# Local attention values with the probabilities as weights, and a feed-forward weight decode per f on VectorE

## The chip, the core and the metric

The kernel runs on one core of a Trainium2 chip. The core has five engines with queues of their own: PE (TensorE, the 128x128 matrix array; its weight loads are listed apart as PEld), VectorE (DVE), ScalarE (ACT), GpSimd (POOL), and SyncE (SP), whose queue issues every DMA of this kernel. Matrix products go to PSUM, eight banks of 128 partitions by 512 float32 columns; all else lives in SBUF. The metric is the device time of one execution in microseconds. A profile shows one execution; its span runs from the first to the last instruction.

## The reference

A batch of 8 with 8 heads of size 64 has 512 local and 32 global tokens. Global queries attend to all 544 keys; local queries attend to the 32 global keys and to local keys at most 32 positions away. The result, of all heads side by side (512 features for each of 4352 tokens), goes through a two-layer feed-forward network with 2048 hidden features.

```python
s_g = scale * np.matmul(q_g, k_all.transpose(0, 1, 3, 2))
out_g = np.matmul(sm(s_g), v_all)
s_ll = scale * np.matmul(q_l, k_l.transpose(0, 1, 3, 2))
mask = np.abs(pos[:, None] - pos[None, :]) <= 32
s_ll = np.where(mask, s_ll, -1e9)
s_lg = scale * np.matmul(q_l, k_g.transpose(0, 1, 3, 2))
a_l = sm(np.concatenate([s_lg, s_ll], axis=-1))
out_l = np.matmul(a_l, np.concatenate([v_g, v_l], axis=2))
...
h = x @ w_in
g = np.maximum(h, 0.0) + alpha * np.minimum(h, 0.0)
return (g @ w_out).astype(np.float32)
```

`sm` is a softmax whose denominator has 1e-9 added.

## The kernel before

Everything is kept transposed: features on partitions, tokens on columns. Two heads make a pair; there are 32 pairs P, four for each batch entry. The feed-forward network runs over 9 groups of tokens: the local tokens of each batch entry (512 columns), and last all global tokens (256 columns). Each group takes 16 steps f, one for each 128 hidden features, so that there are 144 steps t in all, and 10 steps of a prelude ahead of them (t from -10).

In step t, `f1(t)` forms 128 hidden features in one PSUM bank by 12 products of 128x128 weights with 512 columns. Float32 accuracy comes from splitting both factors in a high and a low part (`split`, and `wt`, which holds both parts of the weights) and adding three products. VectorE applies the slope (L291, L292), ScalarE rounds the high part `gh` (L294), GpSimd forms the low part `gl` (L295). `f2` of two steps earlier adds that step's features into four output banks: part 0 (8 products with `gh`) and part 1 (4 with `gl`). Between these stand three places for attention: "pre" ahead of f1, "mid" between f1 and f2's part 0, and "post" between f2's two parts. `plan` (L325 on) puts the attention there: for the local pair P its scores and softmax, two steps later the transposes of the probabilities, three steps later the value products; for the global queries of a pair, every 3.4 steps from t = 16, scores at "mid" of a step and transposes and values at "mid" two steps later.

For a local pair, 16 windows of 32 queries against 128 keys and two heads give 32 products with 32-wide weights (`local_scores`). `local_softmax` masks and negates (L190), takes the minimum (L191), exponentiates on ScalarE in eight pieces with the sums (L193), and multiplies by the reciprocal (L194 to L197). `local_transposes` turns the probabilities on PE and copies them to SBUF. `local_values` (L217) uses the values, 128 keys by 64 features, as weights and streams 32 turned probabilities, 32 products that alternate between the two halves of the array's columns; its result is already transposed and is copied to `x_raw` (L228). `global_values` (L258) turns the global probabilities `sg_sb` into `sgt_sb` and then adds up 5 blocks of keys for each head in one bank. A float32 product appears as two records in the trace.

The weights come as float64 and are turned into float32 bits in the kernel: `load_weights`, `decode_words` (two ScalarE steps, three VectorE steps, one addition on GpSimd, L133 to L140) and `split_weights` (a cast on ScalarE or VectorE, and a subtraction on GpSimd, L150). Of the 32 pieces of 512 columns, 5 are decoded in the prelude and two in each step from t = 0.

The program is ordered by a scheduler that models the engines' times, with priorities by program order; from t = 16 (`PIN`) PE's instructions keep the written order. Every engine and the SP queue take their instructions in order, so a waiting one holds up those behind it. Buffers: tag "s" has two PSUM banks for scores, transposes, values and all global attention from pair 4 on; "h" has two for f1; "o0" to "o3" hold the outputs. `wpool` has 33 buffers of 4 KB a partition.

Of the kernel before, what the change touches and what calls it, by code (L numbers as in the profile page):

```python
# [55 lines left out]
def longformer_ffn(ctx: ExitStack, tc: tile.TileContext, qk, vs, gn, vg, w, alpha, out):  # L56
# [66 lines left out]
    wraw, wmid, wts = {}, {}, {}  # L123

    def load_weights(f, j):
        wraw[f, j] = wpool.tile([128, 1024], U32, tag="w", name="wraw")
        nc.sync.dma_start(wraw[f, j], w[f, j].bitcast(U32))

    def decode_words(f, j):
        words = wraw.pop((f, j)).rearrange("p (n two) -> p n two", two=2)  # L130
# [9 lines left out]
        nc.gpsimd.tensor_tensor(ti, ti, r, op=ALU.add)  # L140
        wmid[f, j] = t

    def split_weights(f, j):
        t = wmid.pop((f, j))
        wt = wpool.tile([128, 2, 512], F32R, tag="w", name="wt")
        if j:
            nc.vector.tensor_copy(wt[:, 0, :], t)  # L147
# [36 lines left out]
    def local_softmax(P):  # L184
        for h in range(2):
# [4 lines left out]
            nc.vector.scalar_tensor_tensor(p, s, -0.125, mask.rearrange("q i n -> q (i n)"), op0=ALU.mult, op1=ALU.add)  # L190
            nc.vector.tensor_reduce(mn, p3, axis=AX.X, op=ALU.min)  # L191
            for i in range(4):
                nc.scalar.activation(p3[:, i], p3[:, i], AF.Exp, bias=mn[:, i : i + 1], scale=-1.0, accum_out=z[:, i : i + 1])  # L193
# [266 lines left out]
```

## Time and profile before

| | us |
|---|---|
| median of 3 runs | 1083.85 (1083.85 to 1089.67) |
| the profiled execution's own time | 1083.33 |
| its span | 1081.5 |
| PE busy, 8752 matmul instructions | 1016.3 (94%) |
| VectorE busy, 1206 instructions | 573.9 (53%) |
| ScalarE busy, 995 instructions | 338.0 (31%) |
| GpSimd busy, 227 instructions | 281.0 (26%) |

How to read the rows that follow: a row of a timeline gives the start, the length, the engine, the line, the operation, the output and inputs by the program's names, the shape and the count; in square brackets stands the idle time ahead of it and what ended it. Matmuls are pipelined and their ends are modelled, so the start of the next batch tells more than the length of one. A row of the groups gives the count, then the busy time, the mean length in ns, and the idle time. A row of the windows gives the stretch and its length, the busy time of PE, PEld, DVE, ACT and POOL with their instructions, the granted PE clock (1.00 is full), the DMA share and GB/s. L78 and L84 are helpers that issue all products and transposes, so the tile names tell them apart.

### The profile page before, as it was taken

Reading aid. Unit: us, or ns where it says so; the run is one execution under the profiler, and the core shown is the slowest. Engines: PE = TensorE matmul, PEld = TensorE weight load, DVE = VectorE, ACT = ScalarE, POOL = GpSimd, SP = SyncE. Lnnn points to the kernel's source line nnn. Section 1 sums busy time; section 2 is a strip of 40 time slices with the busy share of each in tenths; the row PEclk is TensorE's granted clock in tenths of the full one; section 3 lists DMA queues with packets and bytes.
Section 4 is the critical chain, followed back from the end, with each engine's and each line's share of the span. In section 5 each row is a group of like instructions: output and inputs, shape, how many; then the busy total and the mean of one; then the engine's idle time right before and its main releaser. Section 6 shows DMA issues by size and latency. Waiting matters only on the chain.

```text
span 1081.5 us, 21173 instructions
## 1 busy us (share of the span) xinstructions
PE 1016.3 (94%) x8752; PEld 804.9 (74%) x8752; DVE 573.9 (53%) x1206; ACT 338.0 (31%) x995; POOL 281.0 (26%) x227
## 2 busy tenths in 40 slices
PE   6899989899999999999999999999999999999998
PEld 4676566677777777777777777777777777777798
DVE  4579999844445445554454544644453444433322
ACT  3445445332223222422223222422232222311121
POOL 2248777421111121211112112112111212111222
PEclk8698898899999999999999999999999999999999
DMA  9936320243223223333223322333323211200010
GB/s 314 312 143 220 113 89 26 77 128 91 87 76 117 64 86 92 100 119 97 89 88 104 89 63 77 128 89 102 89 89 105 87 44 45 75 24 13 1 40 20
DMA packets 90416, 103.09 MB, mean 95 GB/s; under 512 B 3792, under 2 KB 69840, under 8 KB 90320
## 3 DMA queue, kind: packets, MB, share of 16 engines
q1 hardware_dynamic: 90320, 101.73, 29.9%
q8 instruction: 69, 1.13, 0.4%
q14 instruction: 27, 0.22, 0.1%
HBM read 92.81 MB, written 8.91 MB: 94 GB/s over the span
## 4 chain that ended last, share of the span: by engine, by line
PE 76%; DVE 16%; issue 3%; ACT 2%; DMA 1%; POOL 1%; SPq 0%; DVEq 0%; POOLq 0%; ACTq 0%
PE h_ps L78 31%; PE o L78 31%; PE o_ps L78 5%; DVE g L291 3%; PE pt L84 3%; DVE wt L138 2%; PE s_ps L78 2%; PE gt L78 2%; DVE wt L135 2%; PE g_ps L78 2%; DVE xl L214 1%; DVE p L190 1%; DVE wt L147 1%; DVE sgt_sb L263 1%; ACT p L193 1%
## 5 line engine op out<-in xcount | busy, mean ns | idle before, releaser
L295 POOL TENSOR_TENSOR gl<-g,gh 128x512 fp32r<-128x512 f32 (+1 forms) x144 | 186.0, 1292 | 713.5 <-ACT gh L294 489.8
L78 PE MATMUL h_ps<-xh,wt 128*128 128x512 f32 (+1 forms) x1152 | 358.0, 392 | 5.1 <-POOL wt L150 4.4
L78 PE MATMUL o<-gh,wt 128*128 128x512 f32 (+1 forms) x1152 | 281.8, 386 | 1.6 <-ACT gh L294 1.5
L291 DVE TENSOR_SCALAR g<-h_ps,alpha_sb 128x512 f32<-128x512 f32 (+1 forms) x144 | 103.6, 719 | 319.4 <-PE h_ps L78 296.0
L78 PEld LDWEIGHTS h_ps<-xh,wt 128*128 128x128 f32 x1152 | 209.0, 191 | 52.5 <-issue 8.0
L78 PEld LDWEIGHTS o<-gh,wt 128*128 128x128 f32 x1152 | 203.8, 189 | 41.9 <-ACT gh L294 2.9
L294 ACT CAST gh<-g 128x512 fp32r<-128x512 f32 (+1 forms) x144 | 85.6, 594 | 449.3 <-DVE g L292 369.8
L78 PE MATMUL h_ps<-xl,wt 128*128 128x512 f32 (+1 forms) x576 | 222.6, 387 | 2.0 <-DVE xl L214 2.0
L78 PE MATMUL o<-gl,wt 128*128 128x512 f32 (+1 forms) x576 | 148.9, 380 | 2.1 <-POOL gl L295 2.1
L193 ACT ACTIVATE p<-p,mn 128x128 f32<-128x128 f32 x256 | 99.2, 389 | 103.8 <-DVE mn L191 87.2
L78 PEld LDWEIGHTS h_ps<-xl,wt 128*128 128x128 f32 x576 | 109.9, 191 | 26.4 <-DVE xl L214 4.0
L78 PEld LDWEIGHTS o<-gl,wt 128*128 128x128 f32 x576 | 105.1, 189 | 23.6 <-POOL gl L295 3.5
L292 DVE SCALAR_TENSOR_TENSOR g<-h_ps,g 128x512 f32<-128x512 f32 (+1 forms) x144 | 94.5, 656 | 2.5
L78 PEld LDWEIGHTS o_ps<-pt,vw 128*64 128x64 f32 x2048 | 67.4, 146 | 13.9 <-issue 9.8
L78 PE MATMUL o_ps<-pt,vw 128*64 128x32 f32 x2048 | 71.2, 230 | 1.8 <-DVE pt L99 1.8
L190 DVE SCALAR_TENSOR_TENSOR p<-s_ps,mask 128x512 f32<-128x512 f32 x64 | 41.1, 683 | 49.4 <-PE s_ps L78 49.3
L140 POOL TENSOR_TENSOR wt<-wt,wr 128x512 int32<-128x512 int32 x32 | 44.3, 1385 | 63.6 <-DVE rz L194 24.4
L78 PE MATMUL s_ps<-qk 64*32 64x128 f32 x2048 | 53.3, 295 | 5.5 <-DMA qk<-in_qk_dram 3.5
L78 PE MATMUL gt<-sgt_sb,vg 128*64 128x32 f32 x640 | 24.8, 225 | 34.1 <-DVE sgt_sb L263 34.1
L78 PEld LDWEIGHTS s_ps<-qk 64*32 64x32 f32 x2048 | 35.6, 113 | 28.4 <-issue 18.0
L197 DVE TENSOR_TENSOR p<-p,rz 128x512 f32<-128x512 f32 x60 | 53.4, 891 | 1.9
L78 PEld LDWEIGHTS gt<-sgt_sb,vg 128*64 128x64 f32 x640 | 21.2, 137 | 41.7 <-DVE sgt_sb L263 41.7
(62 smaller groups left out, 752.0 us busy)
## 6 DMA issues: line engine op xcount, KB each, us to landing
vw<-in_vs_dram SPq DMA_DIRECT2D x64, 512.0 KB, 5.1
qk<-in_qk_dram SPq DMA_DIRECT2D x32, 672.0 KB, 4.1
wraw<-in_w_dram SPq DMA_DIRECT2D x32, 512.0 KB, 6.8
vg<-in_vg_dram SPq DMA_DIRECT2D x32, 320.0 KB, 2.9
gn<-in_gn_dram SPq DMA_DIRECT2D x32, 304.0 KB, 2.9
out_dram<-ost SPq DMA_DIRECT2D x32, 256.0 KB, 2.4
out_dram<-ost SPq DMA_DIRECT2D x4, 128.0 KB, 1.8
alpha_sb<-in_alpha_dram SPq DMA_DIRECT2D x1, 8.0 KB, 1.8
```

The costliest lines, as they stand in the source:

```text
L78: ins = nc.tensor.matmul(*a, **k)
L84: ins = nc.tensor.transpose(*a)
L135: nc.vector.tensor_scalar(t, t, CLAMP_LO, CLAMP_HI, op0=ALU.max, op1=ALU.min)
L138: nc.vector.scalar_tensor_tensor(tu, high, 0xC0000000, tu, op0=ALU.bitwise_and, op1=ALU.bitwise_or)
L140: nc.gpsimd.tensor_tensor(ti, ti, r, op=ALU.add)
L190: nc.vector.scalar_tensor_tensor(p, s, -0.125, mask.rearrange("q i n -> q (i n)"), op0=ALU.mult, op1=ALU.add)
L193: nc.scalar.activation(p3[:, i], p3[:, i], AF.Exp, bias=mn[:, i : i + 1], scale=-1.0, accum_out=z[:, i : i + 1])
L197: eng.tensor_tensor(p3, p3, sub_ap(rz, 0, 128, 0, ((1, 4), (0, 128))), op=ALU.mult)
L291: nc.vector.tensor_scalar(g[:, 0:n], h[:, 0:n], 0.0, alpha_sb[:, f : f + 1], op0=ALU.min, op1=ALU.mult)
L292: nc.vector.scalar_tensor_tensor(g[:, 0:n], h[:, 0:n], 0.0, g[:, 0:n], op0=ALU.max, op1=ALU.add)
L294: nc.scalar.copy(gh[:, 0:n], g[:, 0:n])
L295: nc.gpsimd.tensor_tensor(gl[:, 0:n], g[:, 0:n], gh[:, 0:n].bitcast(F32), op=ALU.subtract)
```

## The change

- Local values: the turned probabilities (32 columns) become the weights and the values (64 columns) are streamed, four windows into the four quarters of the array's columns. The result has queries on partitions; it is multiplied by the reciprocal sums there (`xq`), and four transposes in a function of its own, `local_outputs`, bring it to the old layout. The probabilities are no longer scaled. `plan` puts the values at "post" of the step of the transposes, and `local_outputs` at "mid" of the next.
- Global values: the transposes go to "pre" of the step behind the scores, the products to "post" of that step, with both heads in one product of 128-wide weights and 64 columns, of which the copies take each head's own block.
- Weights: both halves of an f are loaded, decoded and split together, 1024 columns a step, with the addition and subtraction on VectorE and the cast on ScalarE. Three f are decoded in the prelude, the others spread over t = 1 to 13.
- Prelude: 7 steps instead of 10, a pair in each; the loads of the four pairs and of three weight tiles are issued ahead, into buffers of the weight pool (17 of 8 KB now). Later pairs have one buffer instead of two for `qk` and for `v`; `gn` and `vg` share three buffers with the decode.

```diff
-NWARM = 12
+NWARM = 9
 WARM = (2, 2)
-NWB = 33
-NST = 22
+NWB = 17
+NST = 21
 ...
-NPRE = 10
+NPRE = 7
 PIN = 16
+PAD = (176, 32)
 LAG = 2
-AHEAD = 6
-EARLY = 6
+NDEC = 3
 ...
-    wraw, wmid, wts = {}, {}, {}
-
-    def load_weights(f, j):
-        wraw[f, j] = wpool.tile([128, 1024], U32, tag="w", name="wraw")
-        nc.sync.dma_start(wraw[f, j], w[f, j].bitcast(U32))
-
-    def decode_words(f, j):
-        words = wraw.pop((f, j)).rearrange("p (n two) -> p n two", two=2)
+    wslot, wmid, wts = {}, {}, {}
+
+    def wide(name, dtype=F32):
+        return work.tile([128, 1024], dtype, tag="dec", name=name, bufs=3)
+
+    def load_weights(f):
+        wslot[f] = wpool.tile([128, 2048], U32, tag="w", name="ws")
+        nc.sync.dma_start(wslot[f], w[f].bitcast(U32))
+
+    def decode_words(f):
+        words = wslot.pop(f).rearrange("p (n two) -> p n two", two=2)
         low, high = words[:, :, 0], words[:, :, 1]
-        t, r = stage("wt"), stage("wr", I32)
+        t, r = wide("wt"), wide("wr", I32)
 ...
         ti = t.bitcast(I32)
-        nc.gpsimd.tensor_tensor(ti, ti, r, op=ALU.add)
-        wmid[f, j] = t
-
-    def split_weights(f, j):
-        t = wmid.pop((f, j))
-        wt = wpool.tile([128, 2, 512], F32R, tag="w", name="wt")
-        if j:
-            nc.vector.tensor_copy(wt[:, 0, :], t)
+        nc.vector.tensor_tensor(ti, ti, r, op=ALU.add)
+        wmid[f] = t
+
+    def split_weights(f):
+        t = wmid.pop(f).rearrange("p (j n) -> p j n", j=2)
+        wt = wpool.tile([128, 2048], F32R, tag="w", name="wt").rearrange("p (j s n) -> p j s n", j=2, s=2)
+        nc.scalar.copy(wt[:, :, 0, :], t)
+        nc.vector.tensor_tensor(wt[:, :, 1, :], t, wt[:, :, 0, :].bitcast(F32), op=ALU.subtract)
+        for j in range(2):
+            wts[f, j] = wt[:, j]
+
+    qks, vws = {}, {}
+
+    def load_qk(P):
+        if P < NPAIR:
+            qks[P] = wpool.tile([128, 2048], F32, tag="w", name="qk")[:, 0 : SL + KS]
         else:
-            nc.scalar.copy(wt[:, 0, :], t)
-        nc.gpsimd.tensor_tensor(wt[:, 1, :], t, wt[:, 0, :].bitcast(F32), op=ALU.subtract)
-        wts[f, j] = wt
-
-    qks, vws = {}, {}
-
-    def load_qk(P):
-        qks[P] = work.tile([128, SL + KS], F32, tag="qk", name="qk", bufs=2)
+            qks[P] = work.tile([128, SL + KS + PAD[1]], F32, tag="qk", name="qk", bufs=1)[:, 0 : SL + KS]
         nc.sync.dma_start(qks[P], qk[P])
 
     def load_v(P):
+        if P < NPAIR:
+            t = wpool.tile([128, 2048], F32, tag="w", name="vw")
+        else:
+            t = work.tile([128, 2048], F32, tag="v", name="vw", bufs=1)
+        vws[P] = t.rearrange("k (e i d) -> k e i d", e=2, i=8)
         for e in range(2):
-            if P < NPAIR:
-                t = wpool.tile([128, 8, 128], F32, tag="w", name="vw")
-            else:
-                t = work.tile([128, 8, 128], F32, tag="v", name="vw", bufs=2)
 ...
-            nc.sync.dma_start(t, src)
-            vws[P, e] = t
-
-    ps_of, pr_of, rz_of, pt_of = {}, {}, {}, {}
+            nc.sync.dma_start(vws[P][:, e], src)
+
+    ps_of, pr_of, z_of, pt_of, xq_of = {}, {}, {}, {}, {}
 
 ...
     def local_softmax(P):
+        z = small("z", 8)
         for h in range(2):
             s = ps_of.pop((P, h))
             p = stage("p")
             p3 = p.rearrange("q (i n) -> q i n", i=4)
-            mn, z, rz = small("mn"), small("z"), small("rz")
+            mn = small("mn")
 ...
             for i in range(4):
-                nc.scalar.activation(p3[:, i], p3[:, i], AF.Exp, bias=mn[:, i : i + 1], scale=-1.0, accum_out=z[:, i : i + 1])
-            nc.vector.tensor_scalar(rz, z, 1e-9, None, op0=ALU.add)
-            nc.vector.reciprocal(rz, rz)
-            eng = nc.gpsimd if P < NPAIR and h == 0 else nc.vector
-            eng.tensor_tensor(p3, p3, sub_ap(rz, 0, 128, 0, ((1, 4), (0, 128))), op=ALU.mult)
+                k = 2 * i + h
+                nc.scalar.activation(p3[:, i], p3[:, i], AF.Exp, bias=mn[:, i : i + 1], scale=-1.0, accum_out=z[:, k : k + 1])
             pr_of[P, h] = p
+        z_of[P] = z
 
 ...
     def local_values(P):
+        o = bank("h" if P < NPAIR else "s", "o_ps")
+        v = vws.pop(P)
+        for i4 in range(4):
+            for h in range(2):
+                for k in range(4):
+                    i = 4 * i4 + k
+                    c = 128 * i4 + 64 * h
+                    matmul(o[32 * k : 32 * k + 32, c : c + 64], pt_of[P, h][:, 32 * i : 32 * i + 32], v[:, i % 2, i // 2, 64 * h : 64 * h + 64], start=True, stop=True)
+        z, rz = z_of.pop(P), small("rz", 8)
+        nc.scalar.activation(rz, z, AF.Copy, bias=1e-9)
+        nc.vector.reciprocal(rz, rz)
+        xq = stage("xq")
+        nc.vector.tensor_tensor(xq.rearrange("q (g d) -> q g d", g=8), o.rearrange("q (g d) -> q g d", g=8), sub_ap(rz, 0, 128, 0, ((1, 8), (0, 64))), op=ALU.mult)
+        xq_of[P] = xq
+
+    def local_outputs(P):
         b, p = divmod(P, NPAIR)
-        o = bank("h" if P < NPAIR else "s", "o_ps")
-        for i in range(NWIN):
-            v = vws[P, i % 2][:, i // 2]
-            for h in range(2):
-                q = slice(32 * i, 32 * i + 32)
-                matmul(o[64 * h : 64 * h + 64, q], v[:, 64 * h : 64 * h + 64], pt_of[P, h][:, q], start=True, stop=True)
+        xq = xq_of.pop(P)
+        ps = bank("h" if P < NPAIR else "s", "xt")
+        for i in range(4):
+            transpose(ps[:, 128 * i : 128 * i + 128], xq[:, 128 * i : 128 * i + 128], ident)
         if P < NPAIR:
-            xs[0, p] = split(o, SL)
+            xs[0, p] = split(ps, SL)
         else:
-            nc.scalar.copy(x_raw[:, p], o)
+            nc.scalar.copy(x_raw[:, p], ps)
 
     gns, vgs, gbank = {}, {}, {}
 
     def load_global(P):
-        gns[P] = work.tile([128, 608], F32, tag="gn", name="gn", bufs=1)
+        gns[P] = wide("gn")[:, 0:608]
         nc.sync.dma_start(gns[P], gn[P])
-        vgs[P] = work.tile([128, 5, 128], F32, tag="vg", name="vg", bufs=1)
+        vgs[P] = wide("vg")[:, 0:640].rearrange("k (y d) -> k y d", y=5)
         nc.sync.dma_start(vgs[P], vg[P])
 
 ...
-    def global_values(P):
-        b, p = divmod(P, NPAIR)
+    def global_transposes(P):
         ps = bank("s", "gt")
 ...
-        v = vgs.pop(P)
+        gbank[P] = ps
+
+    def global_values(P):
+        b, p = divmod(P, NPAIR)
+        v, ps = vgs.pop(P), gbank.pop(P)
         for y in range(5):
-            for h in range(2):
-                matmul(ps[64 * h : 64 * h + 64, 256:288], v[:, y, 64 * h : 64 * h + 64], sgt_sb[:, y, 32 * h : 32 * h + 32], start=(y == 0), stop=(y == 4))
-        nc.scalar.copy(x_glb[:, p, SG * b : SG * b + SG], ps[:, 256:288])
+            matmul(ps[:, 256:320], v[:, y], sgt_sb[:, y], start=(y == 0), stop=(y == 4))
+        for h in range(2):
+            hs = slice(64 * h, 64 * h + 64)
+            nc.scalar.copy(x_glb[hs, p, SG * b : SG * b + SG], ps[hs, 256 + 32 * h : 288 + 32 * h])
 
 ...
     for P in range(NPR):
-        base = 2 * P - NPRE if P < NPAIR else 4 * (P - NPAIR)
+        base = P - NPRE if P < NPAIR else 4 * (P - NPAIR)
         plan(base, "pre", local_scores, P)
         plan(base, "pre", local_softmax, P)
-        plan(base + 2, "pre", local_transposes, P)
-        plan(base + 3, "pre", local_values, P)
-        if P >= 2:
-            prev = base - 2 if P <= NPAIR else base - 4
-            plan(prev, "mid", load_qk, P)
-        if P >= 1:
-            plan(base - 2 if P < NPAIR else base - 1, "post", load_v, P)
+        if P < NPAIR:
+            plan(base + 1, "mid", local_transposes, P)
+            plan(base + 2, "mid", local_values, P)
+            plan(base + 2, "post", local_outputs, P)
+        else:
+            plan(base + 2, "pre", local_transposes, P)
+            plan(base + 2, "post", local_values, P)
+            plan(base + 3, "mid", local_outputs, P)
+            plan(base - 4 if P > NPAIR else -2, "mid", load_qk, P)
+            plan(base - 1, "post", load_v, P)
     for k in range(NPR):
         t = 16 + (17 * k) // 5
         plan(t - 2, "post", load_global, k)
         plan(t, "mid", global_scores, k)
-        plan(t + 2, "mid", global_values, k)
+        plan(t + 1, "pre", global_transposes, k)
+        plan(t + 1, "post", global_values, k)
 
 ...
-    pieces = sorted(((f, j) for f in range(NF) for j in range(2)), key=lambda x: x[0] + 1.5 * x[1])
-    state = [0]
-    done = []
-
-    def weights_step(n):
-        k = state[0]
-        new = list(range(k, min(k + n, len(pieces))))
-        for i in new:
-            if i + AHEAD < len(pieces):
-                load_weights(*pieces[i + AHEAD])
-            decode_words(*pieces[i])
-        state[0] += len(new)
-        done.append([pieces[i] for i in new])
-        if len(done) > 1:
-            for key in done.pop(0):
-                split_weights(*key)
+    state = [0, NDEC]
+
+    def weights_step(t):
+        u = t + NPRE
+        n = NDEC * (u + 1) // NPRE if t < 0 else NDEC + (NF - NDEC) * (t + 1) // (NF - 2)
+        for f in range(state[0], min(n, NF)):
+            if state[1] < NF:
+                load_weights(state[1])
+                state[1] += 1
+            decode_words(f)
+            split_weights(f)
+        state[0] = max(state[0], min(n, NF))
 
 ...
-    load_qk(0)
-    load_v(0)
-    load_qk(1)
-    for k in range(AHEAD):
-        load_weights(*pieces[k])
+    for P in range(NPAIR):
+        load_qk(P)
+        load_v(P)
+        if P < NDEC:
+            load_weights(P)
 ...
-        weights_step(2 if t >= 0 else u % 2 if u < NPRE else 1)
+        weights_step(t)
     assert not at
 
 
 ...
-    w = np.empty((NF, 2, 128, 512), np.float64)
-    w[:, 0] = moe_w_in.reshape(NC, 128, NF, 128).transpose(2, 1, 0, 3).reshape(NF, 128, 512)
-    w[:, 1] = moe_w_out.reshape(NF, 128, DM)
+    w = np.empty((NF, 128, 2, 512), np.float64)
+    w[:, :, 0] = moe_w_in.reshape(NC, 128, NF, 128).transpose(2, 1, 0, 3).reshape(NF, 128, 512)
+    w[:, :, 1] = moe_w_out.reshape(NF, 128, DM)
+    w = w.reshape(NF, 128, 1024)
 ...
```

More of the change, by code (lines that the diff above doesn't have):

```diff
@@ L63, in longformer_ffn @@
     wpool = ctx.enter_context(tc.tile_pool(name="wpool", bufs=NWB))
-    alpha_sb = const.tile([128, NF], F32, name="alpha_sb")
+    alpha_sb = const.tile([128, NF + PAD[0]], F32, name="alpha_sb")[:, 0:NF]
     mask = const.tile([128, 4, 128], F32, name="mask")
@@ L139, in decode_words @@
         ti = t.bitcast(I32)
-        nc.gpsimd.tensor_tensor(ti, ti, r, op=ALU.add)
-        wmid[f, j] = t
-    def split_weights(f, j):
-        t = wmid.pop((f, j))
-        wt = wpool.tile([128, 2, 512], F32R, tag="w", name="wt")
-        if j:
-            nc.vector.tensor_copy(wt[:, 0, :], t)
-        else:
-            nc.scalar.copy(wt[:, 0, :], t)
-        nc.gpsimd.tensor_tensor(wt[:, 1, :], t, wt[:, 0, :].bitcast(F32), op=ALU.subtract)
-        wts[f, j] = wt
+        nc.vector.tensor_tensor(ti, ti, r, op=ALU.add)
[7 more added lines that the diff above has]
+            wts[f, j] = wt[:, j]
     qks, vws = {}, {}
     def load_qk(P):
-        qks[P] = work.tile([128, SL + KS], F32, tag="qk", name="qk", bufs=2)
+        if P < NPAIR:
+            qks[P] = wpool.tile([128, 2048], F32, tag="w", name="qk")[:, 0 : SL + KS]
+        else:
+            qks[P] = work.tile([128, SL + KS + PAD[1]], F32, tag="qk", name="qk", bufs=1)[:, 0 : SL + KS]
         nc.sync.dma_start(qks[P], qk[P])
     def load_v(P):
+        if P < NPAIR:
[3 more added lines that the diff above has]
+        vws[P] = t.rearrange("k (e i d) -> k e i d", e=2, i=8)
         for e in range(2):
-            if P < NPAIR:
-                t = wpool.tile([128, 8, 128], F32, tag="w", name="vw")
-            else:
-                t = work.tile([128, 8, 128], F32, tag="v", name="vw", bufs=2)
             off = (P * KS + 32 * e) * 128
             src = bass.AP(tensor=vs.tensor, offset=off, ap=[[128, 128], [96 * 128, 8], [1, 128]])
-            nc.sync.dma_start(t, src)
-            vws[P, e] = t
-    ps_of, pr_of, rz_of, pt_of = {}, {}, {}, {}
+            nc.sync.dma_start(vws[P][:, e], src)
+    ps_of, pr_of, z_of, pt_of, xq_of = {}, {}, {}, {}, {}
     def local_scores(P):
@@ L328, in longformer_ffn @@
     for P in range(NPR):
-        base = 2 * P - NPRE if P < NPAIR else 4 * (P - NPAIR)
+        base = P - NPRE if P < NPAIR else 4 * (P - NPAIR)
         plan(base, "pre", local_scores, P)
         plan(base, "pre", local_softmax, P)
-        plan(base + 2, "pre", local_transposes, P)
-        plan(base + 3, "pre", local_values, P)
-        if P >= 2:
-            prev = base - 2 if P <= NPAIR else base - 4
-            plan(prev, "mid", load_qk, P)
-        if P >= 1:
-            plan(base - 2 if P < NPAIR else base - 1, "post", load_v, P)
+        if P < NPAIR:
+            plan(base + 1, "mid", local_transposes, P)
+            plan(base + 2, "mid", local_values, P)
+            plan(base + 2, "post", local_outputs, P)
+        else:
+            plan(base + 2, "pre", local_transposes, P)
[3 more added lines that the diff above has]
+            plan(base - 1, "post", load_v, P)
     for k in range(NPR):
```

## The prediction

> **What bounds the kernel now.** I read the page first (the 40 slices), then the windows by stage, then the timeline of single steps.
>
> ```profile
> span 1081.5 us, 21173 instructions
> ...
> DVE  4579999844445445554454544644453444433322
> ...
> PEclk8698898899999999999999999999999999999999
> ...
> 62.50:204.00 141.50, 130.10 (x914) 91.49 (x915) 135.77 (x177) 66.84 (x160) 102.06 (x72) 0.89 0.33 114
> 204.00:1080.00 876.00, 836.52 (x7190) 678.88 (x7190) 407.43 (x969) 245.60 (x751) 160.81 (x128) 1.00 0.26 79
> ```
>
> There are three stages, with three limits. Up to 62.5 us (a prelude, in which the first four head pairs are worked up) nothing is full. From 62.5 to 204 us, while group 0 runs and the weights are decoded, VectorE is busy 135.77 of 141.50 us: it is the bound there (the columns are PE, PEld, DVE, ACT, POOL, clock, DMA, GB/s). From 204 us on PE is busy 836.52 of 876.00 us, and VectorE under half: PE is the bound. So each part of the change is priced in its own stage.
>
> **Prelude.** The change loads all four pairs and three weight tiles at once, one pair per slot, and uses 7 slots instead of 10.
>
> ```profile
> 20.00:40.00 20.00, 16.84 (x218) 12.06 (x216) 9.51 (x19) 7.65 (x24) 3.59 (x3) 0.67 1.11 334
> ...
> 42.03 1.96 PE L78 MATMUL s_ps<-qk 64*32 64x128 f32 x64
> ...
> 47.38 1.28 DVE L190 SCALAR_TENSOR_TENSOR p<-s_ps,mask 128x512 f32<-128x512 f32 x2
> ...
> 60.91 0.58 ACT L213 CAST xh<-o_ps 128x512 fp32r<-128x512 f32 x1 [3.01 <-PE o_ps L78]
> ...
> vw<-in_vs_dram SPq DMA_DIRECT2D x64, 512.0 KB, 5.1
> qk<-in_qk_dram SPq DMA_DIRECT2D x32, 672.0 KB, 4.1
> wraw<-in_w_dram SPq DMA_DIRECT2D x32, 512.0 KB, 6.8
> ```
>
> Before, the scores of pair 3 run at 42.03 and the first FFN product only at 62.5, 20.5 us later, since pair 3's mask step stands until 47.38 behind pair 2's work on VectorE. After, the SP queue issues, without a wait on a buffer, qk, v and w of pairs 0 to 2 and then qk of pair 3: 4 x 672 + 6 x 512 + 3 x 1024 KB = 8832 KB, 9.0 MB, at 334 GB/s 27 us, so by about 30 us; pair 3's v follows 3 us later, and is needed later. If the chain behind the scores keeps its 20.5 us, the first product stands at 51 us; if it shrinks to the 15 us that its steps sum to (2 scores, 2.5 mask and minimum, 3.1 exponentials, 2 transposes, 1 copy, 2 values, 2.5 scaling, turning back and split), at 45 us; VectorE has some 35 us of work to that point (three decodes of 5 us, below, and 20 us of softmax and splits), which fits but leaves little. I take 50 us, **-12.5 us**, with 43 and 58 as ends.
>
> **Group 0: the decode.** Per f the change does each step once on 1024 columns instead of twice on 512, and moves the two GpSimd steps (add, subtract) to VectorE and VectorE's cast to ScalarE.
>
> ```profile
> L197 DVE TENSOR_TENSOR p<-p,rz 128x512 f32<-128x512 f32 x60 | 53.4, 891 | 1.9
> ...
> L138 DVE SCALAR_TENSOR_TENSOR wt<-wraw,wt 128x512 uint32<-128x512 uint32 x32 | 34.7, 1085 | 0.5
> ...
> L135 DVE TENSOR_SCALAR wt<-wt 128x512 f32<-128x512 f32 x32 | 27.2, 851 | 2.8 <-ACT wt L133 2.6
> ...
> L147 DVE CAST wt<-wt 128x512 fp32r<-128x512 f32 x16 | 20.8, 1302 | 0.3
> ...
> L137 DVE TENSOR_SCALAR wt<-wt 128x512 uint32<-128x512 uint32 x32 | 20.1, 629 | 0.2
> ...
> L194 DVE TENSOR_SCALAR rz<-z 128x4 f32<-128x4 f32 x64 | 14.0, 219 | 8.2 <-ACT p L193 7.9
> ...
> 154.86 0.41 DVE L135 TENSOR_SCALAR wt<-wt 128x512 f32<-128x512 f32 x1
> 155.20 0.68 DVE L138 SCALAR_TENSOR_TENSOR wt<-wraw,wt 128x512 uint32<-128x512 uint32 x1
> ```
>
> The decode holds VectorE 34.7 + 27.2 + 20.8 + 20.1 = 102.8 us, though undisturbed its steps take 0.41 (one tensor) or 0.68 (two): 32 x (0.41 + 0.41 + 0.68) + 16 x 0.41 = 55 us. The other 48 us are time in which VectorE stood while GpSimd worked on the same memory: 64 decode steps there and 16 of the subtractions gl, so 0.6 us for each. After: the step of a two-tensor row is 0.53 us for 512 columns (0.68 less 0.15, where 0.41 holds twice the rate, 0.26, and the same 0.15), so 1024 columns take 0.68 (one tensor) or 1.2 (two), and an f takes 2 x 0.68 + 3 x 1.2 = 5.0 us. In group 0 stand 13 of the 16 f: 13 x 5.0 + 16 gl x 0.6 = 75 us, against 102.8 x 27/32 = 87 (27 of 32 pieces): -12. Leaving the probabilities unscaled takes two scalings of 0.89 and four small steps of 0.2 (L194 and its reciprocal) from each pair and gives one of 0.69 and one of 0.18: -1.7 x 4 = -7. VectorE's 135.8 becomes about 117; with its 6 us of idle time the stage is 121 us instead of 141, **-20 us**. ScalarE gets a wide cast per f and stays under half. The lower end is PE's own work, 16 steps of 5.45 (24 products at 0.227, as eight from 260.28 to 262.10 below) and four pairs of 4.0 (scores 1.3, transposes 0.85, values 1.3 and 0.45, below) = 103 us; the upper end is 141, no gain.
>
> **From 204 us on: PE.** PE's instructions stand in written order here, so the timeline gives each batch its price.
>
> ```profile
> 248.13 1.03 PE L84 MATMUL pt<-ident,p 128*128 128x128 f32 x8
> ...
> 248.93 0.71 PE L78 MATMUL h_ps<-xh,wt 128*128 128x512 f32 x2
> ...
> 251.83 0.73 PE L78 MATMUL g_ps<-gn 128*64 128x256 f32 x6
> ...
> 252.50 2.11 PE L78 MATMUL o<-gh,wt 128*128 128x512 f32 x8
> ...
> 255.44 2.06 PE L78 MATMUL o_ps<-pt,vw 128*64 128x32 f32 x64
> ...
> 256.27 0.54 ACT L256 ACTIVATE sg_sb<-sg_sb,gz 128x288 f32<-128x288 f32 x1 [1.29 <-DVE gz L255]
> ...
> 257.43 0.73 PE L78 MATMUL h_ps<-xh,wt 128*128 128x512 f32 x2
> ...
> 260.28 1.98 PE L78 MATMUL o<-gh,wt 128*128 128x512 f32 x8
> ...
> 262.10 1.07 PE L78 MATMUL o<-gl,wt 128*128 128x512 f32 x4
> ...
> 263.09 1.16 PE L78 MATMUL s_ps<-qk 64*32 64x128 f32 x64
> ...
> 264.18 0.73 PE L78 MATMUL h_ps<-xh,wt 128*128 128x512 f32 x2
> ...
> 267.06 0.38 PE L84 MATMUL gt<-ident,sg_sb 128*128 128x128 f32 x2
> ...
> 268.40 0.78 PE L78 MATMUL gt<-sgt_sb,vg 128*64 128x32 f32 x20 [0.96 <-DVE sgt_sb L263]
> ...
> 269.10 2.11 PE L78 MATMUL o<-gh,wt 128*128 128x512 f32 x8
> ...
> 271.05 1.07 PE L78 MATMUL o<-gl,wt 128*128 128x512 f32 x4
> ...
> 357.80 2.11 PE L78 MATMUL o<-gh,wt 128*128 128x512 f32 x8
> ...
> 363.41 0.54 ACT L256 ACTIVATE sg_sb<-sg_sb,gz 128x288 f32<-128x288 f32 x1 [1.06 <-DVE gz L255]
> ```
>
> Local values: 64 records with weights 64 wide fill 255.44 to 257.43, 31 ns each; the scores, 64 records with weights 32 wide, fill 263.09 to 264.18, 17 ns each. The spacing goes with the width of the weights (14 ns per 32 columns), not with the streamed columns (32 against 128). After, the weights are 32 wide and 64 columns stream: nearest to the scores, 1.1 us instead of 2.0. Four transposes come on top, at 0.1 each (eight in 248.13 to 248.93), 0.4 and 0.05 for the change. So -0.45 per pair, x 28 pairs = **-12 us**. Their input is scaled on VectorE behind the values; between lie f2's second part and a whole f1, over 3.6 us, which cover it. The transposed probabilities are now used one step earlier, in the same token; f1 and f2's first part, 4.5 us, cover their two copies.
>
> Global values: now transposes, wait (0.96) and 20 products take 267.06 to 269.10, 2.04 us, and the following f2 part 0.13 more than its 1.82. After: no wait for the transposed weights, since f1 and f2's first part lie between; 2 transposes 0.2, ten records with full weights at 60 ns (17, 31, so 60 for 128 wide) 0.6: 0.8. But the transposes now come one step earlier, and wait for sg_sb. It is ready 4.3 us behind the start of the f2 part (252.50 to 256.81), 6.1 us where the local softmax of the same token is in the way (357.80 to 363.95); of that I take off 1.3 for the scalings that go. PE reaches the transposes 1.82 + 0.91 = 2.75 later, plus what the following token's local work puts ahead of them (nothing, transposes 0.85, scores 1.3, or new values 1.3). By the phase of the 32 tokens: 7 x 2.0, 8 x 0.8, 9 x 0.1, 8 x 0.75 (scores, whose bank must be read first), 27 us, 0.85 each. So 1.65 for 2.17: x 32 = **-16 us**. The ends: no wait at all, -43; the measured 6.1 behind every one, 3.35 of wait each, +64.
>
> ```profile
> 807.95 0.78 PE L78 MATMUL gt<-sgt_sb,vg 128*64 128x32 f32 x20 [2.35 <-DVE sgt_sb L263]
> ...
> 810.00:813.00 3.00, 3.00 (x8) 2.35 (x8) 0.69 (x1) 0.17 (x2) 1.69 (x1) 0.50 0.25 89
> ...
> 448.68 0.77 PE L78 MATMUL gt<-sgt_sb,vg 128*64 128x32 f32 x20 [2.33 <-DVE sgt_sb L263]
> ```
>
> A PE wait can cost more than itself: behind the one of 2.35 us the granted clock was 0.50 for about 3.3 us (1.7 us lost); behind the one of 2.33 us it stayed full. The seven waits of 2 us are thus charged with half of 1.7 each, and with ends of a longer dip 8 us: **+8**. [...]
>
> Other moves: qk and v of later pairs get one buffer instead of two, loaded three steps ahead (over 20 us, landing in 5): nothing. gn and vg share three buffers with the decode; the first is asked for when the decode is done: nothing. **Sum** against the profiled execution: -12.5 - 20 - 12 - 16 + 8 = -52.5 on the span of 1081.5, 1029; its time was 1083.33, 1.8 above the span: **1031 us**. The median of the runs is 1083.85, 0.5 above.
>
> **Rivals.**
> A: VectorE gains nothing in group 0, because the wide steps, with gl against them, and the order on its queue give back what GpSimd no longer takes. The 4% of idle time in that stage speak for it, the 48 us of stalls against. 1031 + 20 = 1051.
> B: slower. The four column groups do not overlap: each product of 64 columns streams for 50 ns (0.1 us for 128 in a transpose) and its weights load 14 ns behind the one before, 64 ns x 64 = 4.1 us instead of 1.1, x 28 = +84: 1115. It turns the sign from 48 ns a record. Against it: 31 ns with weights 64 wide is less than load and product in a row (28 + 25), and g_ps, 4 x 200 + 2 x 25 ns of streaming in two column groups, took 0.67 us. [...]
> C: every wait ahead of the global transposes brings a clock dip: 32 x 1.7 instead of 8 is +46: 1077. The two rows above, one of each kind, leave it open, but waits of 0.96 like that at 268.40 left the clock full, and the stage's mean clock is 1.00.
> D: VectorE is relieved enough that PE sets group 0 too (103 us), and the prelude reaches 43 us: 1031 - 18 - 7 - 6 of dips = 1000.
>
> **How the numbers follow.** Forecast 0.52 (1012 to 1045), A 0.20, B 0.10, C 0.08, D 0.10. About 1%, 11 us, is what a measurement of this kernel can tell from no change. Forecast, A and D are faster: 0.82; C is within 1%: 0.08; B slower: 0.10. Forecast, A (with a prelude of 58 us, up to 1060) and D make up 0.82: the range is 1000 to 1060.
>
> **What would show it.** The first FFN product near 50 us; group 0's stage near 121 us with VectorE still the fullest, and decode steps of 0.68 and 1.2 us; o_ps batches of 1.1 us; transposes gt waiting for sg_sb 0.85 us in the mean, and no wait on sgt_sb. o_ps batches over 3 us, waits of 3 us at gt with a clock of 0.5 behind them, or a group 0 of 140 us would make it wrong.

## The result, and the profile after

The changed kernel takes 1051.8 us (1051.1 to 1059.07, 4 runs); the kernel before, measured beside it, takes 1086.34. The ratio is 0.9695 (95% interval 0.9641 to 0.975): 3% faster. The forecast was 1031 us within 1000 to 1060. One of the four runs took 1059.07, at a slightly lower granted clock (0.974 against 0.981 to 0.984). The profiled execution took 1051.84 us, with a span of 1049.7.

First the page of the changed kernel, then its windows: the prelude in two parts, group 0, and the rest (columns as in the windows above).

```profile
span 1049.7 us, 20450 instructions
...
PE 986.1 (94%) x8548; PEld 792.0 (75%) x8548; DVE 515.4 (49%) x1050; ACT 355.5 (34%) x1027; POOL 187.5 (18%) x159
...
DVE  5999935444454445443454535344454444333322
...
PEclk8799999999999999999999999999999999999999
```

```profile
20.00:40.00 20.00, 13.94 (x272) 10.66 (x272) 18.80 (x29) 15.95 (x47) 0.00 (x0) 0.66 1.08 378
40.00:59.70 19.70, 16.45 (x233) 11.22 (x234) 17.90 (x24) 14.59 (x29) 0.00 (x0) 0.83 0.76 308
59.70:170.50 110.80, 106.98 (x925) 83.02 (x924) 87.57 (x113) 58.20 (x125) 28.59 (x16) 0.98 0.35 121
170.50:1048.00 877.50, 836.57 (x6965) 679.33 (x6964) 380.83 (x871) 258.02 (x806) 155.46 (x128) 1.00 0.25 79
```

VectorE's full stretch has moved from group 0 into the prelude (18.80 of 20 us, 17.90 of 19.7). In group 0 PE is now the fullest engine, 106.98 of 110.80 us, and VectorE has 87.57. From 170 us on nothing looks changed, and that is the surprise.

VectorE's first slope step of a token (L291 before, L312 after) marks the stages. The timeline has it for t = 0 and t = 16, first of the kernel before, then of the changed one, there with the first FFN product ahead:

```profile
65.65 0.75 DVE L291 TENSOR_SCALAR g<-h_ps,alpha_sb 128x512 f32<-128x512 f32 x1 [0.38 <-PE h_ps L78]
...
206.76 0.73 DVE L291 TENSOR_SCALAR g<-h_ps,alpha_sb 128x512 f32<-128x512 f32 x1
```

```profile
58.15 0.73 PE L78 MATMUL h_ps<-xh,wt 128*128 128x512 f32 x2
...
62.94 0.75 DVE L312 TENSOR_SCALAR g<-h_ps,alpha_sb 128x512 f32<-128x512 f32 x1
...
173.15 0.74 DVE L312 TENSOR_SCALAR g<-h_ps,alpha_sb 128x512 f32<-128x512 f32 x1
```

| stage, us | before | after | difference | forecast |
|---|---|---|---|---|
| prelude, to t = 0 | 65.7 | 62.9 | -2.7 | -12.5 |
| group 0, t = 0 to 16 | 141.1 | 110.2 | -30.9 | -20 |
| the rest, to the end of the span | 874.7 | 876.5 | +1.8 | -20 |

The slope step stands behind the first products of its step. By the first FFN product itself, which is what the forecast of the prelude named, the prelude is 4.6 us shorter (62.72 before, 58.15 after).

The first two stages together are right (-33.6 for -32.5), their split is not, and the rest gained nothing. For the rest, this is PE's own time: from the start of each PE group in the timeline to the start of the next, less the idle time in brackets, summed by me from the slope step of t = 16 to PE's last product (the stage's last 4 to 5 us stand behind it). The third column is the experiment g_late, below.

| PE from t = 16 on, us | before | after | g_late |
|---|---|---|---|
| FFN products | 686.0 | 691.0 | 686.8 |
| local values, with the transposes xt | 47.7 | 34.6 | 35.2 |
| global transposes and products | 34.8 | 39.8 | 38.4 |
| scores and local transposes | 65.2 | 68.8 | 66.4 |
| waits | 36.6 | 37.3 | 1.7 |

The changed kernel's rows behind it, from the timeline and then from the groups:

```profile
249.43 1.10 PE L78 MATMUL o_ps<-vw,pt 128*32 128x64 f32 x64
250.46 1.20 PE L78 MATMUL o<-gl,wt 128*128 128x512 f32 x4
251.68 0.44 PE L84 MATMUL gt<-ident,sg_sb 128*128 128x128 f32 x2
...
254.72 0.60 PE L84 MATMUL xt<-ident,xq 128*128 128x128 f32 x4
255.08 2.11 PE L78 MATMUL o<-gh,wt 128*128 128x512 f32 x8
257.02 1.22 PE L78 MATMUL gt<-sgt_sb,vg 128*128 128x64 f32 x10
258.06 1.17 PE L78 MATMUL o<-gl,wt 128*128 128x512 f32 x4
```

```profile
L84 PE MATMUL gt<-ident,sg_sb 128*128 128x128 f32 x64 | 14.0, 300 | 36.6 <-ACT sg_sb L273 26.3 <-DVE p L195 10.0
```

The local batch takes 1.03 us (249.43 to 250.46) and its transposes here 0.36 (0.41 in the mean). The ten global records take 1.04 us (257.02 to 258.06). The wait on the transposed weights is gone, but 36.6 us of waiting for `sg_sb` and for the score bank stand in its place. The FFN products and the scores with their transposes take 8.6 us more than before, by the same sums. A part of that is the change of form between batches, of which there are more now: a second f2 part, 4 products, takes 0.91 us behind the first part, 1.00 behind the global products and 1.03 behind the local ones.

### The profile page after: what moved, and what is told of

Its sections match the earlier page's. It is cut to its first block, busy times and chain, and to the rows that moved or that the text cites. A ratio compares the mean times of both kernels' runs of the same rounds, so it can differ in the third digit from the quotient of the medians.

```text
span 1049.7 us, 20450 instructions
## 1 busy us (share of the span) xinstructions
PE 986.1 (94%) x8548; PEld 792.0 (75%) x8548; DVE 515.4 (49%) x1050; ACT 355.5 (34%) x1027; POOL 187.5 (18%) x159
## 5 line engine op out<-in xcount | busy, mean ns | idle before, releaser
L78 PE MATMUL h_ps<-xh,wt 128*128 128x512 f32 (+1 forms) x1152 | 352.4, 389 | 2.0 <-DVE g L313 1.9
L312 DVE TENSOR_SCALAR g<-h_ps,alpha_sb 128x512 f32<-128x512 f32 (+1 forms) x144 | 103.5, 719 | 298.2 <-PE h_ps L78 292.0
L78 PE MATMUL o<-gl,wt 128*128 128x512 f32 (+1 forms) x576 | 153.0, 387 | 0.0
L78 PEld LDWEIGHTS o<-gl,wt 128*128 128x128 f32 x576 | 101.2, 189 | 18.5
L78 PE MATMUL s_ps<-qk 64*32 64x128 f32 x2048 | 45.5, 289 | 8.4 <-DMA qk<-in_qk_dram 7.8
L245 ACT COPY x_raw<-xt 128x512 f32<-128x512 f32 x28 | 16.4, 585 | 105.8 <-PE xt L84 105.8
L84 PE MATMUL gt<-ident,sg_sb 128*128 128x128 f32 x64 | 14.0, 300 | 36.6 <-ACT sg_sb L273 26.3
L199 ACT ACTIVATION_READ_ACCUMULATOR p<-p,mn 128x1 f32 x256 | 48.3, 189 | 0.0
L99 DVE COPY pt<-pt 128x512 f32<-128x512 f32 x32 | 22.1, 690 | 50.1 <-PE pt L84 47.8
L84 PE MATMUL pt<-ident,p 128*128 128x128 f32 x256 | 40.2, 293 | 4.5 <-ACT pt L97 3.0
L84 PEld LDWEIGHTS gt<-ident,sg_sb 128*128 128x128 f32 x64 | 6.4, 140 | 47.6 <-ACT sg_sb L273 36.0
```

Of the source, the lines that this page charges most:

```text
L78: ins = nc.tensor.matmul(*a, **k)
L84: ins = nc.tensor.transpose(*a)
L99: nc.vector.tensor_copy(dst, src)
L245: nc.scalar.copy(x_raw[:, p], ps)
L312: nc.vector.tensor_scalar(g[:, 0:n], h[:, 0:n], 0.0, alpha_sb[:, f : f + 1], op0=ALU.min, op1=ALU.mult)
```

## The experiments

All are the changed kernel with one edit (g_late_64 with two), timed beside the kernel before; differences are to the changed kernel's 1051.8 us. The kernel before took 1084.1, 1089.43 and 1085.05 us in these three sessions, against 1086.34 beside the changed one, so a difference of a few us needs a trace to support it.

**g_late.** The global transposes go from "pre" of t + 1 to "mid", behind f1.

```diff
-        plan(t + 1, "pre", global_transposes, k)
+        plan(t + 1, "mid", global_transposes, k)
```

> Only the place of the global transposes differs from the changed kernel: mid of the next step instead of pre. Theory W (PE's waits for sg_sb and for a score bank, 36.6 us in all, are what eats the gain behind group 0): sg_sb is ready 4.3 to 6.1 us behind the f2 part, PE arrives at 5.5 or later, so the waits fall below 6 us in all, the products wait nowhere (f2's first part, 1.8 us, covers the 1.0 of the copies), and the time falls by 27 to 37 us, to 1015 to 1025. Rival (the waits hide something else that ends as late, for instance the two score banks now held by others): the waits move to the scores or the products and the time falls by less than 10 us.

1008.08 us (1006.17 to 1009.58), ratio 0.9295 (0.9269 to 0.932): 44 us less. Its rows of the groups:

```profile
L78 PE MATMUL gt<-sgt_sb,vg 128*128 128x64 f32 x320 | 40.0, 272 | 0.4 <-DVE sgt_sb L279 0.4
L84 PE MATMUL gt<-ident,sg_sb 128*128 128x128 f32 x64 | 12.3, 275 | 0.2 <-ACT sg_sb L273 0.2
```

Both waits are gone: f1 covers the softmax in front of the transposes, and f2's first part covers the copies behind them. The gain is larger than the expected 27 to 37 us since the table's other rows fall too: the FFN products by 4.2 us (no stretch at half clock is left), the scores and all other attention batches by about 3.

**g_64.** The global products as before, 20 records with 64-wide weights instead of ten with 128.

```diff
-            matmul(ps[:, 256:320], v[:, y], sgt_sb[:, y], ...)
+            for h in range(2):
+                matmul(ps[64 * h : 64 * h + 64, 256:288], v[:, y, 64 * h : 64 * h + 64], sgt_sb[:, y, 32 * h : 32 * h + 32], ...)
```

> Only the form of the global products differs from the changed kernel: twenty records with weights 64 wide, each head into its half of the columns, instead of ten with weights 128 wide. Theory R (a float32 record with full-width weights costs 0.10 us whatever it streams): the batch shrinks from 1.04 us to 0.70, with 0.12 for each change of the array's division 0.8, so 5 to 11 us less in all, 1041 to 1047. Rival (the batch is bound by the streamed columns or by the accumulation in one bank): no change, within 3 us of 1051.8.

1043.78 us (1043.33 to 1045.31), ratio 0.9623 (0.9596 to 0.9651): 8 us less. Its timeline:

```profile
257.43 0.77 PE L78 MATMUL gt<-sgt_sb,vg 128*64 128x32 f32 x20
258.13 1.21 PE L78 MATMUL o<-gl,wt 128*128 128x512 f32 x4
```

0.70 us for twenty, 35 ns each, against 104 ns for a full-width record of 64 columns: a batch of twice the records costs a third less. The same number of columns streams in both batches, but the narrow records alternate between two halves of the array, so the width and the alternation are not told apart here. The 32 batches are 11.2 us shorter; some of it goes back to the f2 parts around them, and to one more stretch at half clock.

**v_serial.** The 16 local products of one quarter of the array's columns follow each other, instead of taking the quarters in turn.

```diff
-        for i4 in range(4):
-            for h in range(2):
-                for k in range(4):
+        for k in range(4):
+            for i4 in range(4):
+                for h in range(2):
```

> Only the order of the 32 local value products differs from the changed kernel: eight in a row go to the same quarter of the columns, instead of four quarters in turn. Theory C (the quarters overlap, and that is what makes the batch 1.03 us): records of one quarter stream one behind the other, 50 to 64 ns each, so a batch takes 3.2 to 4.1 us and the time rises by 60 to 85 us, to 1110 to 1137. Rival (the batch is bound by the width of the weight loads alone, and the order does not matter): the batch stays near 1.1 us and the time within 5 us of 1051.8.

1107.33 us (1105.81 to 1109.9), ratio 1.0213 (1.0185 to 1.0241): 55.5 us more, a little below the expected range. Its timeline:

```profile
261.80 3.18 PE L78 MATMUL o_ps<-vw,pt 128*32 128x64 f32 x64
264.91 1.20 PE L78 MATMUL o<-gl,wt 128*128 128x512 f32 x4
```

The same 64 records take 3.11 us, 49 ns each, against 16 ns when the quarters alternate. From t = 16 on, where 24 of the 32 pairs stand, the batches cost 50.0 us more (74.7 for 24.7). So the overlap across column groups is real, and the kernel's sign hangs on it: this is rival B's case, reached by order alone, at 49 ns a record instead of B's 64. All 128 rows are used in every record of both runs (128*32 in the rows); only the order of the column groups differs.

**v_old_rest** and **v_old_same.** The old local value products, and the old scaling ahead of them, for pairs 8 to 31. The first (below) adds a small tile `rz4` for the reciprocals, the second takes `rz` there, so that nothing moves in SBUF. `local_outputs` falls away for these pairs.

```diff
+            if P >= 8:
+                rz = small("rz4")
+                nc.vector.tensor_scalar(rz, sub_ap(z, 0, 128, h, ((2, 4),)), 1e-9, None, op0=ALU.add)
+                nc.vector.reciprocal(rz, rz)
+                nc.vector.tensor_tensor(p3, p3, sub_ap(rz, 0, 128, 0, ((1, 4), (0, 128))), op=ALU.mult)
...
+                    matmul(o[64 * h : 64 * h + 64, q], v[:, i % 2, i // 2, 64 * h : 64 * h + 64], pt_of[P, h][:, q], start=True, stop=True)
+            nc.scalar.copy(x_raw[:, p], o)
```

> The local value products of pairs 8 to 31 (the pairs worked up behind group 0) have the old form: values as weights, probabilities scaled on VectorE, no transposes of the result. Theory L (the new form saves 0.45 us of PE a pair): 24 pairs x 0.45 = 11 us more, 1060 to 1065. Rival (the new form gained nothing behind group 0, which is why that stretch did not get shorter): within 4 us of 1051.8.

1093.0 us (1091.47 to 1094.75), ratio 1.0079 (1.0052 to 1.0106): 41 us more, far outside. The 12 products of an f1 took 2.79 us there where nothing else disturbs them, against 2.72 in the changed kernel, and the placement of the tiles had changed too. That is why the second followed.

> The same edit as v_old_rest (old local value products for pairs 8 to 31), but the reciprocals use the small tile that is there already, so that no other tile in SBUF moves. In v_old_rest f1's twelve products took 2.95 us in the mean, against 2.85 in the changed kernel. Theory A (a product's speed depends on where its operands lie in SBUF, and the new small tile had shifted them): f1 is back at 2.85, and what is left is 11 us for the form, 12 for the longer waits for sg_sb (48 us in that run against 37) and some 6 for clock dips: 1075 to 1084. Rival (the form itself slows the products around it): 1090 or more as in v_old_rest, 1093.

1081.8 us (1079.3 to 1085.18, 6 runs), ratio 0.9945 (0.9918 to 0.9973): 30 us more, as theory A had it. (The 2.95 and 2.85 us quoted there include stretches at half the clock; undisturbed they are 2.79 and 2.72, and here 2.72 again.) Its rows of the timeline and of the groups:

```profile
252.80 2.06 PE L78 MATMUL o_ps<-pt,vw 128*64 128x32 f32 x64
254.79 1.20 PE L78 MATMUL o<-gl,wt 128*128 128x512 f32 x4
```

```profile
L84 PE MATMUL gt<-ident,sg_sb 128*128 128x128 f32 x64 | 14.2, 305 | 49.0 <-ACT sg_sb L286 37.1 <-DVE p L195 11.8
```

By the same sums as in the table, the old form costs 13.1 us, the waits 13.2 (the scalings on VectorE are back; that these make `sg_sb` later is argued) and the first FFN layer's products 7.7 (more stretches at half clock); other batches give some 5 back. So, as long as these waits stand, the new form of the local values is worth 30 us, less than half of it in its own batches.

**nopad.** `PAD = (0, 0)`: the two tiles that the change widens, without any use of the added columns, get their old width.

```diff
-PAD = (176, 32)
+PAD = (0, 0)
```

> The two pads of the change (176 columns behind alpha_sb, 32 behind the single qk buffer) are zero; nothing else differs from the changed kernel, but the tiles behind them lie elsewhere. Theory A (the place in SBUF sets the products' speed): f1's twelve products take 2.9 us or more in place of 2.85 and the time rises by 8 to 25 us. Rival (the pads do nothing for the time): within 4 us of 1051.8.

1059.64 us (1059.22 to 1060.53), ratio 0.9739 (0.971 to 0.9768): 7.8 us more, just under the expected 8. The changed kernel's own longest run (1059.07) is as long, so the times alone do not show it; the traces do. One undisturbed f1 of the changed kernel, then one of nopad, from the timelines (the start of the first product, and of the f2 part behind the last):

```profile
537.57 0.62 PE L78 MATMUL h_ps<-xh,wt 128*128 128x512 f32 x2
...
540.29 1.98 PE L78 MATMUL o<-gh,wt 128*128 128x512 f32 x8
```

```profile
542.90 0.62 PE L78 MATMUL h_ps<-xh,wt 128*128 128x512 f32 x2
...
545.68 2.02 PE L78 MATMUL o<-gh,wt 128*128 128x512 f32 x8
```

2.72 against 2.78 us, and 1.98 against 2.02 in the next batch: identical instructions run 2% slower when their operands lie elsewhere in SBUF. Summed as in the table, the FFN products are 8.3 us longer (699.3 for 691.0), the whole difference. It is not the session or the chip: dec_pool and v_old_same, timed beside nopad, show 2.72 us. Nor is it a gain against the kernel before, whose undisturbed f1 takes 2.72 us too.

**dec_pool.** The addition and the subtraction of the decode back on GpSimd, still 1024 columns wide.

```diff
-        nc.vector.tensor_tensor(ti, ti, r, op=ALU.add)
+        nc.gpsimd.tensor_tensor(ti, ti, r, op=ALU.add)
...
-        nc.vector.tensor_tensor(wt[:, :, 1, :], t, wt...
+        nc.gpsimd.tensor_tensor(wt[:, :, 1, :], t, wt...
```

> The addition and the subtraction of the weight decode are back on GpSimd, 1024 columns each; all else is the changed kernel. Theory S (GpSimd's steps make VectorE stand: 0.6 us for each of 1.3 us before, so 1.2 for each of 2.6 now): VectorE loses 2 x 1.2 us of own work per f and gets 2 x 1.2 of standing back, so the stretch up to the first product of group 1 changes by less than 8 us, and the move alone was worth little. Rival F (VectorE stands for the whole GpSimd step, 2.6 each): 16 x 2.8 = 45 us more there. Rival N (no standing): 20 us less there, down to PE's own work.

1076.69 us (1076.3 to 1077.44), ratio 0.9896 (0.9866 to 0.9925): 25 us more, outside all three. The groups, first of the changed kernel, then of dec_pool:

```profile
L141 DVE SCALAR_TENSOR_TENSOR wt<-ws,wt 128x1024 uint32<-128x1024 uint32 x16 | 21.0, 1312 | 0.1
L143 DVE CUSTOM_DVE_ANT_0 wt<-wt,wr 128x2048 uint16<-128x2048 uint16 x16 | 19.9, 1242 | 0.3
L150 DVE TENSOR_TENSOR wt<-wt 128x1024 fp32r<-128x1024 f32 x16 | 19.5, 1216 | 0.0
...
L138 DVE TENSOR_SCALAR wt<-wt 128x1024 f32<-128x1024 f32 x16 | 11.4, 712 | 3.4 <-ACT wt L136 3.3
L140 DVE TENSOR_SCALAR wt<-wt 128x1024 uint32<-128x1024 uint32 x16 | 10.9, 681 | 0.1
```

```profile
L150 POOL TENSOR_TENSOR wt<-wt 128x1024 fp32r<-128x1024 f32 x16 | 41.4, 2586 | 17.3 <-ACT wt L149 17.3
L143 POOL TENSOR_TENSOR wt<-wt,wr 128x1024 int32<-128x1024 int32 x16 | 38.0, 2376 | 34.3 <-DVE wt L141 25.0 <-ACT wt L136 4.9 <-ACT pt L97 3.2
L141 DVE SCALAR_TENSOR_TENSOR wt<-ws,wt 128x1024 uint32<-128x1024 uint32 x16 | 35.6, 2222 | 0.4
L138 DVE TENSOR_SCALAR wt<-wt 128x1024 f32<-128x1024 f32 x16 | 23.6, 1472 | 17.6 <-ACT wt L136 17.6
...
L140 DVE TENSOR_SCALAR wt<-wt 128x1024 uint32<-128x1024 uint32 x16 | 18.1, 1132 | 0.3
```

The three steps that stay on VectorE go from 21.0 + 11.4 + 10.9 = 43.3 to 77.3 us: 34 us over 32 GpSimd steps, 1.1 us for each. So the stall that the prediction inferred is real. The kernel before shows it too: one L135 step takes 1.49 us (152.03) beside a GpSimd step that runs from 151.52 to 153.24, another 0.41 (154.86) with none beside it. What the two engines contend for was not tried. But VectorE's decode is not longer in all (77.3 against 82.7 us). What is longer is the way of an f through the engines, 2.4 and 2.6 us for a GpSimd step in place of 1.2: t = 16 came at 194.73, 21.6 us later, of which 12.8 us arise before t = 0 already. That this longer way is the cause is argued from the lengths, not tried.

**g_late_64.** The edits of g_late and g_64 together.

> Both edits of the global values: transposes at mid of the next step (1008.1) and twenty 64-wide records (8.0 us less in g_64). If the two are independent, as PE has hardly a gap left behind group 0: 998 to 1002. Rival (the change of the array's division at mid and post costs back what the narrower weights save): 1005 to 1010.

1000.33 us (998.15 to 1001.54), ratio 0.9188 (0.9153 to 0.9223). The two gains add up (43.7 and 8.0 for 51.5), and this version beats both kernels.

**dec_late.** The changed kernel starts each of f 3, 4 and 5 in the prelude already, as VectorE's queue was filled with them by the scheduler. Here the first VectorE step of f 3 to 15 keeps its place in the written order.

```diff
-        nc.vector.tensor_scalar(t, t, CLAMP_LO, CLAMP_HI, op0=ALU.max, op1=ALU.min)
+        ins = nc.vector.tensor_scalar(t, t, CLAMP_LO, CLAMP_HI, op0=ALU.max, op1=ALU.min)
+        if f >= NDEC:
+            tc.keep_in_program_order(ins)
```

> The changed kernel, but the first VectorE step of the decode of f 3 to 15 is held behind VectorE's work of its own token, so that the decodes of f 3, 4 and 5 no longer stand on VectorE's queue ahead of the first FFN product. Theory Q: the first product (58.15 us in the changed kernel) was late since VectorE, busy 36.7 of the 39.7 us from 20 us on, also did these three decodes of 5.2 us there. Then it comes at 45 to 50 us, step 16 stays at 170 to 176 us (173.2), since the same decodes now stand in group 0, and the time is 1048 to 1055 us (1051.8). Rival L: loads and the chain behind the scores set the first product. Then it stays at 55 to 58 us, the three decodes come on top of group 0, and the time is 1060 to 1068 us.

1057.76 us (1056.67 to 1060.05), ratio 0.9749 (0.9711 to 0.9787): 6 us more, between the two. The first FFN product comes at 53.83 instead of 58.15. Windows and PE's timeline:

```profile
40.00:56.80 16.80, 15.40 (x239) 10.56 (x240) 7.04 (x13) 7.83 (x29) 0.00 (x0) 1.00 0.60 238
140.00:160.00 20.00, 18.13 (x105) 13.49 (x98) 19.76 (x24) 11.77 (x28) 5.32 (x3) 1.00 0.17 51
```

```profile
44.61 0.85 PE L78 MATMUL s_ps<-qk 64*32 64x128 f32 x22 [0.23 <-ACT pt L97]
...
48.20 0.40 PE L78 MATMUL s_ps<-qk 64*32 64x128 f32 x2
48.53 0.50 PE L78 MATMUL warm<-idle 128*128 128x512 f32 x1
48.96 1.10 PE L78 MATMUL o_ps<-vw,pt 128*32 128x64 f32 x64
...
53.83 0.39 PE L78 MATMUL h_ps<-xh,wt 128*128 128x512 f32 x1
```

VectorE now idles for 9.8 of 16.8 us ahead of group 0 and is full near its end (19.76 of 20). Step 16 stays (173.65), but the step behind it, 182.1 us in the changed kernel, comes 3.9 us later, and 1.4 us more are lost far behind. At both places stands a stretch at half clock that the changed kernel has not, 1.7 us each, so only some 2 us are a delay of the work itself. So decoding ahead used idle time of VectorE, at 4.3 us of delay for the first product, and cost nothing in the end. The other 3.8 us to the forecast 50 are PE's order: the last prelude pair's value products (48.96) stand behind pair 4's scores (44.61 to 48.5), which I had not counted in the chain. That part is read from the trace and was not tried.

## Why the prediction was right, and where it failed

The direction and the two mechanisms that carry the gain were right: VectorE is relieved of the decode, and the products with narrow weights overlap (16 ns a record for 49, v_serial). The total of 1052 us for 1031 owes something to luck, since errors offset each other in pairs, as the stages show.

**Prelude, -12.5 forecast, -4.6 measured by the first product (-2.7 by the slope step).** The first product came at the far end of the range, 58 us. The chain of the prediction counted three decodes; VectorE had six on its queue (dec_late: 4.3 us), and PE had pair 4's scores.

**Group 0, -20 forecast, -30.9 measured.** An f costs VectorE 82.7 / 16 = 5.17 us, as forecast (5.0), in steps of 0.7 and 1.2 to 1.3 us. Against the kernel before, 512 columns more cost 0.27 us with one tensor (0.68 for 0.41) and 0.54 with two (1.22 for 0.68), the rates that the forecast took. But with three decodes out of the way early and VectorE free of its GpSimd stalls (1.1 us for a wide step, dec_pool), PE became the bound (106.98 of 110.80 us), against my "VectorE still the fullest". That is rival D's mechanism, without its prelude of 43 us. Held in order (dec_late), the stage is 116.9 us, nearer to the forecast 121, with VectorE (108.5) and PE (108.3) equally full. (The prediction's own terms, 117 us busy and 6 idle, make 123.) So the errors of the prelude and of group 0 offset each other in part because the same decodes moved from one to the other: dec_late gives 6.2 us back to the first and takes 6.7 from the second. A part of the gain may also be the clock, which the prediction did not price in this stage: PE ran at half clock for 30.7 us of it before and for 3.4 us after. That was not told apart.

**Local values, -12 forecast for 28 pairs, which is -10.8 for 24; -13.1 measured** for the 24 pairs in this stage: 1.03 and 0.41 us in the mean where 1.1 and 0.45 stood. Taking the price from the row with the same width of weights held, and rival B is excluded by v_serial.

**Global values, -16 forecast: the step that failed.** Transposes and products took 39.8 us instead of 32 x 0.8 = 25.6: ten full-width records take 1.04 us, not 0.6 (g_64). I had drawn a line through the paces of 32- and 64-wide weights, 17 and 31 ns, and read 60 off it; it was 104. Both paces come from batches in which column groups alternate, and v_serial shows 49 ns for 32-wide records that don't; a full-width record has nothing to alternate with. That fits, but it was not told apart from the width. And the waits were 36.6 us, not 27, 10.0 of them for the score bank. One of these is shown here, from the timeline:

```profile
528.30 0.54 ACT L273 ACTIVATE sg_sb<-sg_sb,gz 128x288 f32<-128x288 f32 x1
529.88 1.29 DVE L195 SCALAR_TENSOR_TENSOR p<-s_ps,mask 128x512 f32<-128x512 f32 x2
530.72 0.41 PE L84 MATMUL gt<-ident,sg_sb 128*128 128x128 f32 x2 [2.81 <-DVE p L195]
530.88 0.70 PE L78 MATMUL h_ps<-xh,wt 128*128 128x512 f32 x2
```

`sg_sb` is ready at 528.84, but the transposes need a bank that the local mask step frees only after 529.88: 2.81 us, where the phase was charged with 0.75. Together these two terms are 14.2 + 9.6 = 24 us, as much as the 22 us that the stage fell short. That the two agree is luck in part: the 8 us charged for clock dips did not come (one stretch more than before, 1.7 us), but the FFN products and the scores, which the prediction put at nothing, took 8.6 us more. g_late shows what the lost step was worth: the wait could be removed by one place in the order.

**Clock dips, +8 forecast.** Two were seen from group 0's end on, about 1.7 us each. One of them, and the row above for contrast:

```profile
859.83 0.53 PE L84 MATMUL gt<-ident,sg_sb 128*128 128x128 f32 x2 [1.49 <-DVE p L195]
860.01 1.20 PE L78 MATMUL h_ps<-xh,wt 128*128 128x512 f32 x2
861.01 0.63 PE L78 MATMUL h_ps<-xl,wt 128*128 128x512 f32 x1
```

After a wait of 1.49 us two products take 1.20 us, and the granted clock is 0.50 from 859.98 to 863.40; after one of 2.81 they take 0.70, the full pace, at a clock of 1.00. So rival C (a dip at each wait) is excluded.

What picks the waits was not shown. Their length alone does not: 1.49 us, and 2.35 in the kernel before, had half clock behind them, 2.81, and 2.33 in the kernel before, did not. In the traces of these two kernels each stretch at half clock, but for the one that runs into the end of the program, lasted 3.41 us or a whole multiple of it: 3.41 to 17.07 before, 3.41 and 6.83 after.

**Not in the prediction:** the padding, worth 7.8 us (nopad). It was read as a detail of the layout and not priced. It avoids a loss: with it, f1 keeps the pace that it has in the kernel before. Rival A (no gain in group 0) is excluded by the stage's 110 us, though its 1051 us is the time that came out, by another way.

## What to carry to other kernels

A wait moved to another instruction isn't removed: look for the place in the order where a long batch stands between producer and consumer on both sides (44 us here). Price a record from a row with weights of the same width and the same order of column groups (16, 49 and 104 ns for 64 columns here); don't extend a line beyond the widths measured. When a few per cent matter, compare the pace of identical batches between two kernels before crediting an edit: a tile's place alone made 7.8 us.

## What the runs showed of the hardware that was not expected

- The pace of float32 records with small streams: with 64 columns, 16 ns with weights 32 wide when the four column groups alternate, 49 ns in one group after another, and 104 ns with weights 128 wide; with 32 columns, 35 ns with weights 64 wide in two groups.
- The same 12 products of 512 columns take 2.72 or 2.78 us with the operands in other places in SBUF. Which address matters was not tried.
- A GpSimd step of 2.4 to 2.6 us lengthens VectorE's decode steps by about 1.1 us in all (dec_pool).
- A wait of 1.49 us on PE was followed by 3.41 us at half the clock, one of 2.81 us by none. So its length alone does not decide it; what does was not shown.
